# GroupNorm over 128 samples: fifteen small loads added to the SP queue between the last stores

## The chip, the cores and the metric

The kernel runs on one core of one Trainium2 chip. The metric is device time in microseconds (us) of one execution, where lower is better. Besides the timed runs there is one profiled execution of the kernel before; every number read from a view belongs to that execution.

## What is computed

The reference normalises each of 128 samples in 32 groups of 32 channels with 32x16 pixels, and then scales and shifts each channel. Input and output are bfloat16, `x` of 128x1024x32x16, `g` and `b` of 1024.

```python
def reference(x, g, b):
    G = 32
    B, C, H, W = x.shape[0], x.shape[1], x.shape[2], x.shape[3]
    xr = x.reshape(B, G, C // G, H, W)
    mu = xr.mean(axis=(2, 3, 4), keepdims=True)
    var = ((xr - mu) ** 2).mean(axis=(2, 3, 4), keepdims=True)
    xn = (xr - mu) / jnp.sqrt(var + 1e-5)
    xn = xn.reshape(B, C, H, W)
    return xn * g[None, :, None, None] + b[None, :, None, None]
```

## The kernel before

**Tiling.** One tile holds 4 samples times 32 groups, which makes 128 partitions, and each partition holds one whole group: 32 channels of 512 pixels, 16384 bfloat16 values, 32 KB. So there are NT = 32 tiles of 4 MB, and each is loaded once, normalised in place and stored once. Six buffers (`SLOTS` = 6) are used in turn; tile `i` lives in slot `(i + FIRST) % 6` with `FIRST` = 4.

**The compute engines.** For each tile TensorE adds up the 32 blocks of 512 columns by multiplying them with a unit matrix (L209, L193). ScalarE takes a rough mean of the first channel (L217) and sums squared differences from it in four instructions of 4096 columns (L228). VectorE makes mean, variance and the scale and shift of each channel from these (L244 to L284) and rewrites the tile with 32 instructions of 512 columns (L294). The last of the 32 raises the slot's semaphore `done`.

**The DMA program.** Every DMA is issued by SP, in program order, on one queue. SP issues the load of tile 0, two loads that bring `g` and `b` to 128 partitions (L148 and L149; 128 rows of 64 bytes each, one semaphore for both), and the loads of tiles 1 to 5. Then, for each tile `i`, it waits for `done` and issues the store (L141); from tile 1 to tile 26 it also waits until the store of tile `i - 1` has landed and then issues the load of tile `i + 5` into that slot (L136). Stores 27 to 31 have no load between them. Each load and each store has one semaphore per slot that rises by 16 when the DMA has landed. SP waits for nothing else: it is an instruction stream of its own, and what stands behind a waiting instruction on SP is issued later.

**The end.** Behind the last store SP raises `gone` (L156), for which GpSimd waits before it clears the range of the kernel's semaphores (L334), and then SP waits for the landing of the last store of each slot (L158). Behind that come only the few instructions with which the program ends.

The store and load steps in the code:

```python
for i in range(NT):
    store(i)
    if i >= 1 and i + SLOTS - 1 < NT:
        load(i + SLOTS - 1)
sp.sem_inc(s_gone, 1)
```

Of the kernel before, what the change touches and what calls it, by code (L numbers as in the profile page):

```python
# [11 lines left out]
BF16 = mybir.dt.bfloat16  # L12
# [10 lines left out]
def kernel(  # L23
# [20 lines left out]
    NT = B0 // NS  # L44
# [8 lines left out]
    x_v = x.rearrange("(t n) (q k) h w -> t (n q) (k h w)", n=NS, q=G)  # L53
# [8 lines left out]
    def sb(name, shape, dtype):  # L62
        return ctx.enter_context(nc.sbuf_tensor(name, shape, dtype))
# [3 lines left out]
    def sem(name):  # L67
        all_sems.append(nc.alloc_semaphore(name))
        return all_sems[-1]
# [16 lines left out]
    ja = sb("ja", [P, HW], BF16)  # L86
    js = sb("js", [P, SQ], BF16)
    jd = sb("jd", [P, MM_FREE], BF16)
    jv = sb("jv", [P, SQ_PARTS], F32)

    def small(name, n=1):
# [13 lines left out]
    def sems(name):  # L105
        return [sem(f"{name}{j}") for j in range(SLOTS)]
# [11 lines left out]
    s_scl = sems("scl")  # L118
    s_bia = sems("bia")
    s_done = sems("done")  # L120
    s_gb = sem("gb")
    s_gbf = sem("gbf")
    s_eps = sem("eps")
# [6 lines left out]
    sp, pe, act, dve, pool = nc.sync, nc.tensor, nc.scalar, nc.vector, nc.gpsimd  # L130

    def load(i):
        j, n = (i + FIRST) % SLOTS, i // SLOTS
        if n > 0:
            sp.wait_ge(s_store[j], 16 * n)
        sp.dma_start(out=xs[j][:], in_=x_v[i]).then_inc(s_load[j], 16)  # L136

    def store(i):
        j, n = (i + FIRST) % SLOTS, i // SLOTS
        sp.wait_ge(s_done[j], n + 1)  # L140
        sp.dma_start(out=o_v[i], in_=xs[j][:]).then_inc(s_store[j], 16)  # L141
# [10 lines left out]
    for i in range(NT):  # L152
        store(i)
        if i >= 1 and i + SLOTS - 1 < NT:
            load(i + SLOTS - 1)
    sp.sem_inc(s_gone, 1)  # L156
    for j in range(SLOTS):
        sp.wait_ge(s_store[j], 16 * len(range((j - FIRST) % SLOTS, NT, SLOTS)))  # L158
# [6 lines left out]
        out=half[:],  # L165
        in_=ones[:],
# [8 lines left out]
        out=eye[:],  # L175
        in_=half[:],
# [188 lines left out]
```

## Time and profile before

| | |
|---|---|
| three timed runs | 632.34, 633.8 and 633.92 us; median 633.8 us |
| the profiled execution, its own time | 633.28 us |
| its span, first to last instruction | 631.6 us |
| outside the span | 1.68 us |
| queue of the SP DMAs: share of the 16 DMA engines' span | 98.9% |
| bytes read and written | 134.23 MB and 134.22 MB, 425 GB/s over the span |
| ScalarE / VectorE / TensorE busy | 519.4 / 394.9 / 287.4 us |

How to read it: a busy share is an average over the span, and an engine that is 82% busy can still have time to spare at the end. The core's DMAs are carried by 16 DMA engines. The trace holds, for each packet that one of these engines moved, its start, its size and its duration, though not which engine moved it; a tile's row is one packet of 32 KB, so each engine carries 8 packets of each tile. It also holds each increment by which a DMA engine reports to the DMA's semaphore that its part has landed: 16 increments for each load and store. In the groups of the page, "SPq" is SP's instruction stream, and an issue's duration is the time in which SP handled that one instruction; the transfer itself comes later.

### The profile page before, as it was taken

To read this page: it belongs to the slowest core of one execution; us is meant where nothing else is said; L and a number is where in the kernel's file an instruction comes from. 1 tells how busy PE (TensorE), PEld (TensorE's weight loads), DVE (VectorE), ACT (ScalarE), POOL (GpSimd) and SP (SyncE) were. 2 spreads that over 40 slices of the span, in tenths; PEclk is the share of its full clock that TensorE was granted. 3 is DMA by queue.
4 is the path that set the end of the run, shared out by engine and by line. 5 is a ranking of instruction groups with operands and counts; after the bars stand their busy time and mean duration, and the time that the engine had idled before them with its cause. 6 is when DMAs were issued, how large, how long until landed. Compare 5 with 4: busy or idle time off the path is not lost.

```text
span 631.6 us, 2995 instructions
## 1 busy us (share of the span) xinstructions
PE 287.4 (46%) x1024; PEld 3.3 (1%) x32; DVE 394.9 (63%) x1316; ACT 519.4 (82%) x354; POOL 0.8 (0%) x6
## 2 busy tenths in 40 slices
PE   1967605553255532455324654346553455533400
PEld 0000000000000000000000000000000000000000
DVE  0177777666666677777555775556765557755560
ACT  2999999999999999997879887889887898888800
POOL 0000000000000000000000000000000000000000
PEclk9999758756787667876678776777766787667755
DMA  8999999999999999999999999999999999999995
GB/s 363 432 430 417 436 436 432 430 430 434 428 432 432 432 432 432 430 432 430 430 434 434 436 432 432 438 434 436 430 431 434 434 432 432 434 432 432 432 432 235
DMA packets 9484, 268.50 MB, mean 425 GB/s; under 512 B 1288, under 2 KB 1288, under 8 KB 1288
## 3 DMA queue, kind: packets, MB, share of 16 engines
q1 hardware_dynamic: 9480, 268.46, 98.9%
q14 instruction: 3, 0.02, 0.0%
q8 instruction: 1, 0.02, 0.0%
HBM read 134.23 MB, written 134.22 MB: 425 GB/s over the span
## 4 chain that ended last, share of the span: by engine, by line
DMA 73%; ACT 18%; DVE 4%; issue 1%; SPq 1%; DVEq 0%; ACTq 0%
DMA out_dram<-x 67%; ACT js L228 17%; DMA x<-in_x_dram 7%; DVE x L294 3%; ACT ja L217 1%; SPq L136 1%; ACT std L237 0%; DVE jv L268 0%; DVE nd L259 0%; DVE d L255 0%; DVE bia L284 0%; DVE scl L280 0%; DVEq L58 0%; DVE rstd L278 0%; DVEq L254 0%
## 5 line engine op out<-in xcount | busy, mean ns | idle before, releaser
L228 ACT ACTIVATE js<-x,nshift 128x4096 bf16<-128x4096 bf16 x128 | 474.7, 3708 | 4.1
L294 DVE TENSOR_SCALAR x<-x,scl,bia 128x512 bf16<-128x512 bf16 x1024 | 333.7, 406 | 1.2
L193 PE MATMUL ps<-x,eye 128*128 128x512 bf16 x992 | 275.3, 447 | 0.0
L209 PE MATMUL ps<-x,eye 128*128 128x512 bf16 x32 | 18.6, 581 | 303.8 <-DMA x<-in_x_dram 303.8
L255 DVE TENSOR_TENSOR d<-negmean,nshift 128x1 f32<-128x1 f32 x32 | 5.1, 159 | 167.7 <-ACT js L228 167.7
L217 ACT ACTIVATE ja<-x 128x512 bf16<-128x512 bf16 x32 | 20.0, 624 | 48.7 <-DMA x<-in_x_dram 48.0
L244 DVE TENSOR_SCALAR_CACHE_REDUCE jd<-ps 128x512 bf16<-128x512 f32 x32 | 22.0, 686 | 16.4 <-PE ps L193 16.3
L237 ACT ACTIVATE std<-var,eps_t 128x1 f32<-128x1 f32 x32 | 9.4, 295 | 25.8 <-DVE jv L268 25.8
L228 ACT ACTIVATION_READ_ACCUMULATOR js<-x,nshift 128x1 f32 x128 | 23.9, 186 | 0.0
L278 DVE RECIPROCAL rstd<-std 128x1 f32<-128x1 f32 x32 | 5.2, 164 | 11.6 <-ACT std L237 11.6
L284 DVE SCALAR_TENSOR_TENSOR bia<-scl,negmean,bet 128x32 f32<-128x32 f32 x32 | 8.1, 252 | 1.1
L280 DVE TENSOR_SCALAR scl<-gam,rstd 128x32 f32<-128x32 f32 x32 | 7.7, 241 | 1.1
L186 DVE CAST gam<-gam_b 128x32 f32<-128x32 bf16 x1 | 0.2, 181 | 12.9 <-DMA bet_b<-in_b_dram 12.9
L268 DVE TENSOR_SCALAR_CACHE_REDUCE jv<-sq,nd 128x4 f32<-128x4 f32 x32 | 7.0, 217 | 1.1
L259 DVE TENSOR_SCALAR nd<-d 128x1 f32<-128x1 f32 x32 | 6.8, 214 | 1.1
L209 PEld LDWEIGHTS ps<-x,eye 128*128 128x128 bf16 x32 | 3.3, 103 | 578.7 <-DMA x<-in_x_dram 578.7
L217 ACT ACTIVATION_READ_ACCUMULATOR ja<-x 128x1 f32 x32 | 6.0, 187 | 0.0
L268 DVE DVE_READ_ACCUMULATOR jv<-sq,nd 128x1 f32 x32 | 2.7, 83 | 0.0
L244 DVE DVE_READ_ACCUMULATOR jd<-ps 128x1 f32 x32 | 2.6, 82 | 0.0
L184 ACT ACT_TABLE_LOAD x1 | 1.3, 1283 | 1.0 <-ACTq L58 1.0
L161 DVE MEMSET eps_t<- 128x1 f32 x1 | 0.1, 59 | 1.1 <-ACTq L58 1.1
L164 POOL TENSOR_SCALAR_AFFINE_SELECT half<-ones 128x128 bf16<-128x128 bf16 x1 | 0.3, 292 | 0.9 <-DVE ones L162 0.9
(8 smaller groups left out, 1.2 us busy)
## 6 DMA issues: line engine op xcount, KB each, us to landing
x<-in_x_dram SPq DMA_DIRECT2D x32, 4096.0 KB, 29.2
out_dram<-x SPq DMA_DIRECT2D x32, 4096.0 KB, 38.3
gam_b<-in_g_dram SPq DMA_DIRECT2D x1, 8.0 KB
bet_b<-in_b_dram SPq DMA_DIRECT2D x1, 8.0 KB
```

The source lines that it names most:

```text
L136: sp.dma_start(out=xs[j][:], in_=x_v[i]).then_inc(s_load[j], 16)
L193: return pe.add_instruction(mybir.InstMatmult(name=nc.get_next_instruction_name(), ins=[pe.lower_ap(rhs), first.ins[1]], outs=[first.outs[0]],
L209: m = pe.matmul(out=ps[j][:], lhsT=eye[:], rhs=xs[j][:, 0:MM_FREE], start=True, stop=False)
L217: act.activation(out=ja[:], in_=xs[j][:, 0:HW], func=ACT.Identity, scale=-1.0 / HW, accum_out=nshift[j][:],).then_inc(s_shift[j], 1)
L228: act.activation(out=js[:], in_=xs[j][:, k * SQ : (k + 1) * SQ], func=ACT.Square, bias=nshift[j][:], scale=1.0, accum_out=sq[j][:, k : k + 1],
L237: act.activation(out=std[j][:], in_=var[j][:], func=ACT.Sqrt, bias=eps_t[:], scale=1.0).then_inc(s_std[j], 1)
L244: dve.tensor_scalar(out=jd[:], in0=ps[j][:], scalar1=-inv_n, scalar2=None, op0=ALU.mult, op1=ALU.add, accum_out=negmean[j][:],).then_inc(s ...
L259: dve.tensor_scalar(out=nd2[j][:], in0=d[j][:], scalar1=d[j][:], scalar2=-1.0, op0=ALU.mult, op1=ALU.mult,).then_inc(s_nd2[j], 1)
L268: dve.tensor_scalar(out=jv[:], in0=sq[j][:], scalar1=inv_n, scalar2=nd2[j][:], op0=ALU.mult, op1=ALU.add, accum_out=var[j][:],).then_inc(s ...
L280: dve.tensor_scalar(out=scl[j][:], in0=gam[:], scalar1=rstd[j][:], scalar2=None, op0=ALU.mult).then_inc(s_scl[j], 1)
L284: dve.scalar_tensor_tensor(out=bia[j][:], in0=scl[j][:], scalar=negmean[j][:], in1=bet[:], op0=ALU.mult, op1=ALU.add,).then_inc(s_bia[j], 1)
L294: v = dve.tensor_scalar(out=xs[j][:, k * HW : (k + 1) * HW], in0=xs[j][:, k * HW : (k + 1) * HW], scalar1=scl[j][:, k : k + 1], scalar2=bi ...
```

## The change

Right behind the store of tile 28 (`NT - 4`), which is the fourth store from the end, SP issues fifteen loads. Load number `k` brings the first 32 values (64 bytes) of the first `k` rows of tile 0 into a tensor of its own, `k` partitions by 32 values. Together these are 120 rows of 64 bytes. No instruction reads the fifteen tensors. Each load has a semaphore of its own. SP waits for these fifteen semaphores behind the store of tile 31, ahead of raising `gone`. The semaphores lie in the range that GpSimd clears at the end. Nothing is removed, and the order of all the other instructions on all engines stays as it was.

```diff
@@ -86,6 +86,7 @@
     jd = sb("jd", [P, MM_FREE], BF16)
+    few = [sb(f"few{k}_", [k, 32], BF16) for k in range(1, 16)]
     jv = sb("jv", [P, SQ_PARTS], F32)
@@ -118,6 +119,7 @@
     s_done = sems("done")
+    s_few = [sem(f"few{k}_") for k in range(1, 16)]
     s_gb = sem("gb")
@@ -153,6 +155,11 @@
         store(i)
         if i >= 1 and i + SLOTS - 1 < NT:
             load(i + SLOTS - 1)
+        if i == NT - 4:
+            for k in range(1, 16):
+                sp.dma_start(out=few[k - 1][:], in_=x_v[0][0:k, 0:32]).then_inc(s_few[k - 1], 16)
+    for v in s_few:
+        sp.wait_ge(v, 16)
     sp.sem_inc(s_gone, 1)
```

## The prediction

> **What bounds the kernel now.** I read the page's 40 slices first, then the chain that ended last, then SP's waits and issues from 540 us on, and last the DMA packets of two short stretches. A change of 0.3% (1.9 us) either way is about what a measurement of this kernel can tell from none.
>
> ```profile
> DMA  8999999999999999999999999999999999999995
> ...
> DMA packets 9484, 268.50 MB, mean 425 GB/s; under 512 B 1288, under 2 KB 1288, under 8 KB 1288
> ...
> DMA 73%; ACT 18%; DVE 4%; issue 1%; SPq 1%; DVEq 0%; ACTq 0%
> ```
>
> The DMA engines are over 90% busy in every slice but the first and the last, and DMA makes up 73% of the chain. The queue never runs dry: the bytes set the pace. SP is not what is late, as its own waits from 540 us on show (line, waited for: us, times, longest):
>
> ```profile
> SPq L141 <- DVE x L294: 55.3, 3, 19.0
> SPq L158 <- DMA out_dram<-x: 19.5, 3, 9.6
> ```
>
> SP waits three times for a tile from VectorE (stores 29, 30, 31), up to 19.0 us each, and at the end 19.5 us for stores to land. Yet these late issues cost nothing: store 31 is issued at 610.27 us, and the increments of store 30 still land from 613.85 to 620.57 us. Everything issued from 553 us on stands behind some four tiles of transfers, of about 9.7 us each.
>
> The end has a shape of its own. This is the DMA view of the last 10 us (each column 0.25 us):
>
> ```profile
> DMA  9966033360309003090003600030000000000000
> GB/s 524 786 262 262 0 131 131 131 262 0 131 0 393 0 0 131 0 393 0 0 0 131 262 0 0 0 131 0 0 0 0 0 0 0 0 0 0 0 0 33
> DMA packets 48, 1.02 MB, mean 102 GB/s; under 512 B 16, under 2 KB 16, under 8 KB 16
> ```
>
> The full rate ends near 623 us, and then single packets trickle on. The trace's increments say the same: of store 31's sixteen, eleven land between 623.52 and 624.09 us, and the other five at 625.10, 627.40, 629.17, 629.32 and 630.24. **The end is set by one DMA engine that is 6.7 us behind the first**; SP's last wait ends at its 630.24. Its lag can be followed back through all 64 tile transfers, since it is always at least 0.7 us more than the second slowest's from the second on (2.2 us at load 1, 3.6 at 72 us, 6.5 at 333 us). So work added to that engine's share moves the end by its whole length, and work of up to 0.9 us on any other engine moves nothing.
>
> **The change part by part.** It removes nothing. It adds fifteen issues on SP, 120 rows of 64 bytes with their increments in the queue, fifteen waits on SP, and fifteen semaphores to clear.
>
> *Issues on SP.* The rows nearest to them are SP's first DMAs (start, duration) and store 28 with the store behind it:
>
> ```profile
> 0.98 0.39 SPq L136 DMA_DIRECT2D x<-in_x_dram  x1
> 1.43 0.72 SPq L148 DMA_DIRECT2D gam_b<-in_g_dram  x1
> 2.20 0.56 SPq L149 DMA_DIRECT2D bet_b<-in_b_dram  x1
> 2.81 9.10 SPq L136 DMA_DIRECT2D x<-in_x_dram  x5
> ...
> 553.74 18.14 SPq L141 DMA_DIRECT2D out_dram<-x  x2
> ...
> 571.54 0.33 SPq L141 DMA_DIRECT2D out_dram<-x  x1
> ```
>
> Store 28 is issued at 553.74 us (0.50 us), and store 29 waits for VectorE until 571.54: 17.3 us in which SP does nothing. Fifteen issues cost between 15 x 0.33 = 5.0 us (the shortest store) and 15 x 0.72 = 10.8 us (the `g` load). I take 0.56, the later of the two 64-byte-row loads: 8.4 us. They end at 562.6 us and are hidden under VectorE's work on tile 29. One issue went otherwise: the first of the five loads at 2.81 took 6.34 us, right behind 256 rows of 64 bytes. By rows, 120/256 of that is 3.0 us, and 8.4 + 3.0 = 11.4 us still fits. If every small load were held for 6.34 us, SP would come to store 29 only at 554.2 + 95.1 = 649 us, and the end would be near 680: that is the far bound. I set it aside since the loads issued right behind the 6.34 took 1.21, 0.44, 0.44 and 0.49 us, with more in flight each time.
>
> With that cover gone there is a second one. Behind store 28 the queue holds work until its own landing (594.49 us for the first engine, 601.20 for the slowest), so store 29 may be issued as late as some 594 us, 22 us after its place now, before any engine runs dry.
>
> *Packets.* The fifteen loads stand behind store 28 and ahead of store 29 in the queue, and a load of `k` rows needs `k` packets of 64 bytes and some increments. The stretch where one DMA engine begins to move the rows of `g`, 12.43 to 12.50 us, in columns of 1.75 ns:
>
> ```profile
> DMA  0030003000300030003000700930003000300070
> ...
> DMA packets 13, 0.03 MB, mean 477 GB/s; under 512 B 12, under 2 KB 12, under 8 KB 12
> ```
>
> A small packet starts every fourth column, so every 7 ns, with no gap for a read or a write to come back. The whole of `g` and `b`, 256 rows and 8 increments, is through between 12.43 and 13.44 us. The record has ten increments for the two loads: two at 2.53 and 3.18 us, right behind their issue, and eight with the data, four for each load. So four DMA engines carried them, 66 packets each. If one engine gets a row of every one of the fifteen loads, it gets 15 rows and 15 increments: 30 x 7 = 210 ns. Does the slowest engine get them? At load 1, right behind `g` and `b`, the four that are latest (0.61, 0.70, 1.38 and 2.19 us) stand apart from the rest (up to 0.41), as four that had 66 small packets, 0.47 us, more would. So the slowest is likely one of the four that `g` and `b` used. If the small loads begin with the same ones, it gets 12 to 15 of the fifteen: 0.17 to 0.21 us, **0.2 us**. If it is none of them, the cost is 0.
>
> *What the 7 ns may hide.* In `g` one increment followed 32 rows; now one follows each row on the busiest engine. Upper bound: two engines of the four report `g` at 13.10 and 13.21 us, and `b`, 33 packets later, at 13.34 and 13.45, each 0.24 us on. So one increment can't hold up what is behind it for more than 0.24 us, and fifteen not more than 3.6 us. The lower bound is 0. I take the 7 ns, for a second row speaks for it: the slowest engine's increments for stores 30 and 31 are 9.67 us apart, with 8 packets of median 1.213 us between them (9.70 us), so an increment among large packets leaves no gap at all.
>
> A rule that speaks against this: the Trainium skill, "DMA: Bandwidth & Descriptors", section "Anatomy of one DMA", puts a fixed cost of about 2.0 us on each DMA. Taken as a price of the queue it would make 15 x 2.0 = 30 us, an end near 664 us. The same section says that most of it is the delay until the completion is reported, and the row of `g` and `b` agrees: two whole DMAs passed one engine in 0.47 us.
>
> Which engine gets how much is told by the same page, section "Why a DMA increments its semaphore by 16 and not by 1": a load of `k` rows goes to the lowest-numbered `k` engines. No view of this trace numbers the engines; by the rule the first one would have 15 rows.
>
> *Waits and clearing.* SP's fifteen waits stand behind store 31's issue (610.27 + 0.33 us). By then the small loads have landed (about 601.4 us). Semaphore instructions of L158 take 17 to 28 ns: 15 x 0.028 = 0.42 us, up to 1.1 us with the 0.07 us between neighbours at the end. This lies beside store 30's landing, for which SP now waits until 620.59 us. `gone` comes 0.4 to 1.1 us later, and with it the range clear, 0.59 us at 610.7, some 18 us before the end. Cost 0; without that cover 1.1 us.
>
> **Sum.** 633.28 (span 631.6 plus 1.68 around it) + 0.2 = 633.5 us for this execution. The median of the three runs is 633.8, which is 0.5 above the execution, and the changed kernel is timed in such runs: 633.8 + 0.2 = **634.0 us**.
>
> **Rivals.**
>
> *A small load holds its engine (slower).* If an increment right behind a 64-byte row has to wait for that row to land, and the next row waits for it, the place is the slowest engine's queue between stores 28 and 29. At the bound of 0.24 us a pair, 15 pairs make 3.6 us: 637.4. At the full delay from the last increment's packet (629.90) to its landing (630.24), 0.34 us, it is 5.1 us: 638.9. It decides from 1.9 / 15 = 0.13 us a pair. For it: this pattern is not in the trace. Against it: the 7 ns, and the missing gap.
>
> *SP is held until the queue is dry.* If the fifteen loads fill something that holds SP past 601.2 us, the slowest engine idles. Starting again costs 1.0 us from issue (0.98) to the first packet (2.01 us) and about 0.6 us for the longer first packet (1.79 against 1.21): some 635.6 us, and more the longer SP is held. For it: the 6.34 us issue. Against it: SP had eight DMAs in flight then and went on, and the hold would have to last 47 us.
>
> *Faster.* The lag of 6.7 us grew by chance-like steps; if another execution has 2 us less, the time falls below 632. The runs (632.34 to 633.92) show no such fall, and nothing in the change makes one.
>
> *The change does nothing at all*, because the slowest engine gets no small rows: 633.8 us, inside the forecast.
>
> **How the numbers follow.** Forecast, with the loads that do nothing: 0.74, 632.3 to 635.5. Held engine: 0.15. SP held: 0.06. Faster by over 0.3%: 0.05. So faster 0.05, same 0.74, slower 0.15 + 0.06 = 0.21. The range goes from 632.3, the lowest run, to 637.4, the bound of 0.24 us a pair; left out are the dearer part of the held engine, the longer holds of SP and the faster case, under 0.2 together.
>
> **What would show it.** Right: fifteen small issues of 0.3 to 0.7 us between 554.2 and 566 us on SP; store 29 still issued right behind VectorE's last instruction on its tile; small packets between store 28's and store 29's on each engine at some 7 ns; the lag of the last engine up by 0.2 us at most between these two stores; no wait worth naming for the small loads. Wrong: the last engine's lag jumping by microseconds there, or store 29 issued after 590 us, or other engines joining the late five.

## The result and the profile after

The changed kernel takes 633.91 us (median of 20 runs, 633.34 to 637.66) against 632.32 us of the kernel before in the same measurement (20 runs, 631.55 to 634.04). The ratio is 1.0026, with a 95% interval of 1.0018 to 1.0034, so the change costs 1.6 us (1.1 to 2.1). That is within 0.3%, as forecast, but it is clear of zero, and the working had 0.2 us. That the forecast's 634.0 us was met so closely is luck: the cost was 1.4 us higher than worked out, and the kernel before now came out 1.5 us lower than the 633.8 that the prediction started from. With either error alone it would have been about 1.5 us off.

The profiled execution of the changed kernel took 634.31 us with a span of 632.6 us, 1.0 us longer than before. Its DMA totals, from the page:

```profile
DMA packets 9725, 268.51 MB, mean 424 GB/s; under 512 B 1528, under 2 KB 1528, under 8 KB 1528
```

240 small packets are new, 120 rows and 120 increments. SP's issues and waits around them (start, duration; then who waited for whom, in total, times, longest):

```profile
552.60 0.96 SPq L143 DMA_DIRECT2D out_dram<-x  x2
553.60 9.31 SPq L160 DMA_DIRECT2D few_<-in_x_dram  x15
570.93 0.37 SPq L143 DMA_DIRECT2D out_dram<-x  x1
```

```profile
SPq L143 <- DVE x L301: 46.2, 3, 19.2
SPq L165 <- DMA out_dram<-x: 20.5, 3, 9.6
```

The fifteen issues fill 9.3 us of a stretch in which SP waited for VectorE anyway; store 29 is still issued when VectorE is done. SP's wait for VectorE shrinks from 55.3 to 46.2 us, by just these 9 us, and its wait for the last stores grows from 19.5 to 20.5: the microsecond sits in the DMA engines. The DMA view of the last 10 us shows it:

```profile
DMA  9999096060630306303063033330033300000000
GB/s 524 786 393 393 0 524 262 0 262 0 262 131 0 131 0 262 131 0 131 0 262 131 0 131 131 131 131 0 0 131 131 131 0 0 0 0 0 0 0 0
```

Before, the last packets were thinly spread and the last one started at 628.5 us; now several engines are late together, with packets up to about 630 us. Where it happened is told by the trace's increments (first, and last, of the sixteen of each store, us):

```
             before             after
store 28     594.49 .. 601.20   594.42 .. 600.90
store 29     604.18 .. 610.89   604.39 .. 612.05
store 31     623.52 .. 630.24   623.75 .. 631.37
```

In the kernel before the last engine needs 9.69 us from store 28 to store 29. Now it needs 11.16, and after that the old 9.7 again: 1.47 us are lost once, where the small loads stand. The last engine was 0.3 us earlier at store 28 in this execution, so the end moves by 1.13 us from 630.24.

The small packets themselves run as forecast. A stretch in which one engine moves its rows, 600.55 to 600.72 us, in columns of 4.25 ns:

```profile
DMA  1911011011011010110110110110119190110190
...
DMA packets 31, 0.20 MB, mean 1161 GB/s; under 512 B 25, under 2 KB 25, under 8 KB 25
```

A row and an increment follow every three columns, so a pair takes 13 ns, and 12 pairs are through by 600.71 us. But their increments land far more slowly. Of this engine's twelve loads (those of 4 to 15 rows) they land at

```
601.08 601.27 601.45 601.63 601.83 602.02 602.21 602.40 602.59 602.77 602.95 603.13
```

that is every 0.186 us, fourteen times the pitch of the packets. This is the row that the trace of before did not have.

The large packets behind the small ones say the same. A packet of 32 KB lasts 1.21 us, and in the kernel before none that starts between 594 and 606 us lasts more than 1.25. In the changed kernel six that start between 599 and 606 us do (start, duration, us):

```
600.11 1.96    602.06 1.81
600.24 2.17    602.41 1.70
600.72 1.90    602.61 1.76
```

In each line the second packet starts where the first ends, so each line is one engine. The last line starts right behind the twelve pairs that were through by 600.71 us: this engine takes up the next tile while its small loads are still being reported (until 603.13), and its two packets last 1.2 us longer than two ordinary ones. With the 0.16 us of the small packets that is 1.4 of the 1.47 us lost.

### The profile page after: what moved, and what is told of

Same layout as the page of the kernel before. It is cut to its first block, busy times and chain, and to the rows that moved or that the text cites. A ratio compares the mean times of both kernels' runs of the same rounds, so it can differ in the third digit from the quotient of the medians.

```text
span 632.6 us, 3001 instructions
## 1 busy us (share of the span) xinstructions
PE 288.0 (46%) x1008; PEld 3.3 (1%) x32; DVE 394.9 (62%) x1316; ACT 519.3 (82%) x354; POOL 0.8 (0%) x6
## 4 chain that ended last, share of the span: by engine, by line
DMA 73%; ACT 18%; DVE 4%; issue 1%; SPq 1%; DVEq 0%; ACTq 0%
DMA out_dram<-x 66%; ACT js L235 17%; DMA x<-in_x_dram 7%; DVE x L301 3%; ACT ja L224 1%; SPq L138 1%; ACT std L244 0%; DVE jv L275 0%; DVE nd L266 0%; DVE d L262 0%; DVE bia L291 0%; DVE scl L287 0%; DVEq L58 0%; DVE rstd L285 0%; DVEq L261 0%
## 5 line engine op out<-in xcount | busy, mean ns | idle before, releaser
L251 DVE TENSOR_SCALAR_CACHE_REDUCE jd<-ps 128x512 bf16<-128x512 f32 x32 | 21.9, 685 | 15.6 <-PE ps L200 15.5
```

What stands on the lines that cost most here:

```text
L251: dve.tensor_scalar(out=jd[:], in0=ps[j][:], scalar1=-inv_n, scalar2=None, op0=ALU.mult, op1=ALU.add, accum_out=negmean[j][:],).then_inc(s ...
```

## The experiments

The theories, with the numbers that the profile after suggested:

- **A**: on one DMA engine, increments of successive small loads are held about 0.18 us apart. The engine goes on with the packets behind them meanwhile, which hides the first 0.8 us or so; only the rest is lost. An engine with n pairs loses n x 0.18 - 0.8 us.
- **B**: each small row has a price of about 0.12 us, whatever stands behind it.
- **C**: the cost is in SP's fifteen issues, semaphores and waits, not in the DMA engines.
- **D** (formed after the first four runs): a fixed price of 0.13 us for each pair, with nothing hidden.

All variants change only the number, the shape or the place of the loads (the runs with thirty and with eight loads also let two unused outputs share their space, to make room). Shown of the code are the lines that matter, against the kernel before. Where a loss is named "between stores 28 and 29", it is the mean, over the sixteen increments in order, of the time from store 28 to store 29 less the 9.68 us of the kernel before.

**Two loads of 128 rows.**

```diff
+    rows = [128] * 2
+    few = [sb(f"few{k}_", [n, 32], BF16) for k, n in enumerate(rows)]
...
+        if i == NT - 4:
+            for k, n in enumerate(rows):
+                sp.dma_start(out=few[k][:], in_=x_v[0][0:n, 0:32]).then_inc(s_few[k], 16)
```

> Two loads of 128 rows of 64 bytes instead of the fifteen, at the same place: every DMA engine gets 16 rows but only 2 increments. Theory A (each increment behind small rows holds the writing side of its engine for about 0.18 us until the rows have landed, of which the first 0.8 us in a row are hidden): 2 x 0.18 is below 0.8, so only the packets themselves, 18 x 7 ns = 0.1 us; 0.0 to 0.3 us over the kernel before. Theory B (each small row costs its engine some 0.12 us, whatever stands behind it): 16 x 0.12 = 1.9 us over the kernel before.

Ratio 1.0006 (0.9997 to 1.0015): +0.4 us, -0.2 to 0.9. The loss between stores 28 and 29 is 0.13 us. Sixteen rows on every engine cost next to nothing when only two increments stand behind them: B falls.

**Fifteen loads of 16 rows.** As above, with `rows = [16] * 15`.

> Fifteen loads of 16 rows each: every DMA engine gets 15 rows and 15 increments. Theory A: 15 x 0.18 - 0.8 = 1.9 us over the kernel before, on the late engines and on the others alike; their first landings of store 29 move by as much as the last. Theory B: 15 x 0.12 = 1.8 us. Theory C (the cost is in the fifteen issues, semaphores and waits of SP, not in the engines): as the changed kernel, 1.6 us, and no shift of the landings between stores 28 and 29.

Ratio 1.0037 (1.0025 to 1.0050): +2.3 us, 1.6 to 3.2. The loss is 1.98 us, the first increment moves by 1.95 and the last by 2.00: every engine loses the same. As many rows on each engine as in the run before, less one, but fifteen increments instead of two.

**Five loads of 16 rows.** `rows = [16] * 5`.

> Five loads of 16 rows each: every DMA engine gets 5 rows and 5 increments. Theory A: 5 x 0.18 = 0.9 us on the writing side, nearly all of it hidden: 0.1 to 0.2 us over the kernel before. Theory B (a price for each row, nothing hidden): 5 x 0.12 = 0.6 us. Theory C: a third of 1.6, 0.5 us.

Ratio 1.0004 (0.9995 to 1.0012): +0.25 us, -0.3 to 0.8. By itself that excludes neither 0.1 nor 0.5 us; the trace's loss of 0.16 us does tell, and is A's.

**Fifteen loads of one row.** `rows = [1] * 15`.

> Fifteen loads of one row each: if a load of k rows uses the first k engines, always the same first one, a single engine gets 15 rows and 15 increments, and SP issues, waits and clears exactly as in the changed kernel. Theories A and B: that engine loses 1.9 us; in the changed kernel's profile the engine with all fifteen pairs landed among the first ones, with 5 to 6 us to spare, so the end does not move: 0.0 us (up to 1.9 us in an execution in which that engine happens to be the last). Theory C (issues, semaphores, waits): 1.6 us, as the changed kernel.

Ratio 1.0001 (0.9992 to 1.0010): +0.1 us, -0.5 to 0.6. SP issues, waits and clears as often as in the changed kernel, and nothing is lost: C falls. One engine alone reports the fifteen loads. In this execution it was not among the first, as I had thought from the changed kernel's profile, but 3.7 us behind them; its increments land from 598.50 to 601.05, 0.182 us apart, and from store 28 (598.32) to store 29 (609.95) it loses 1.95 us. It had 2.8 us to spare, and the end does not move. This one engine gives the numbers of A more sharply: 15 x 0.182 = 2.73 us of holds, 1.95 of them lost, so **0.78 us hidden**. Its next large packet starts at 598.18 us, when none of the fifteen has been reported, and lasts 2.36 us, the one behind it 1.74, and then they last 1.21 again. So the engine does go on meanwhile; that this is what hides the 0.78 us fits, but no run tests it by itself.

**Thirty loads of 16 rows.** `rows = [16] * 30`.

> Thirty loads of 16 rows each, so 30 rows and 30 increments on every DMA engine; to make room, the unused output of the rough mean shares the space of the unused output of the squares. Theory A (0.182 us for each pair on the writing side, the first 0.78 us hidden): 30 x 0.182 - 0.78 = 4.7 us later between stores 28 and 29 on every engine, and as much over the kernel before. Theory D (a fixed price of 1.95 / 15 = 0.13 us for each pair, nothing hidden): 3.9 us.

Ratio 1.0094 (1.0079 to 1.0110): +5.9 us, 5.0 to 7.0. The loss is 4.71 us against A's 4.7 and D's 3.9. The timed runs show more than that. In the profile the last engine lost 5.18 us, and its increments were 0.19 us apart, which makes 30 x 0.19 - 0.78 = 4.9; the remainder of about a microsecond (0.1 to 2.1) is open. SP was not the reason in this profile, although its issues grew long:

```profile
L161 SPq DMA_DIRECT2D few_<-in_x_dram x30: 422/926/2949, 552.6 to 586.6; - x30
```

The columns are the shortest, median and longest issue in ns. From the 22nd on they take 1.5 to 2.9 us, and stores 29 and 30 are issued at 589.1 and 591.1 us, 18 us late for store 29, yet before any engine has run dry.

**One load of 16 rows behind each of fifteen stores.**

```diff
         store(i)
+        if 12 <= i < 27:
+            k = i - 12
+            sp.dma_start(out=few[k][:], in_=x_v[0][0:16, 0:32]).then_inc(s_few[k], 16)
         if i >= 1 and i + SLOTS - 1 < NT:
```

> Fifteen loads of 16 rows, as in the run that cost 2.3 us, but one behind each of the stores 12 to 26 instead of all behind store 28. Theory A: a single hold of 0.18 us is below the 0.78 us that are hidden, and the 9.7 us until the next one let the writing side catch up: only the packets, 15 x 0.013 = 0.2 us over the kernel before. Theory D (a fixed price for each pair, wherever it stands): 1.95 to 2.3 us.

Ratio 1.0010 (1.0001 to 1.0019): +0.6 us, 0.1 to 1.2. The same fifteen loads that cost 2.3 us in a row cost 0.6 when they are spread, one every 19.4 us; the interval takes in A's 0.2 and excludes D's 1.95. The trace agrees: from store 11 to store 28 the increments take 319.85 us on the mean, against 319.80 in the kernel before (319.67 to 319.96 in the runs that change nothing in this stretch). So the hidden part is there for each hold anew when they stand apart.

**Fifteen loads of 128 rows.** `rows = [128] * 15`.

> Fifteen loads of 128 rows of 64 bytes: 15 increments on every DMA engine as with 16 rows, but 120 rows. Theory A (the increments are held): successive increments 0.21 us apart, as in the run with two loads of 128 rows, so 15 x 0.21 - 0.78 = 2.4 us over the kernel before. Theory B (each row has its price): 120 x 0.13 = 15.6 us. If SP is held by so many rows, its issues take longer than 0.6 us each, but have 40 us before an engine runs dry.

Ratio 1.0043 (1.0029 to 1.0057): +2.7 us, 1.8 to 3.6. Eight times the rows of the run with 16, and nowhere near B's 15.6 us. It is not a clean test of A, though. The 0.21 us that the expectation took from the run with two loads is not what the last engine showed there, which was 0.19. Here the last engine's increments are 0.18 to 0.20 us apart but for two gaps of 0.43 and 0.37 us, whose reason is open; it loses 2.84 us instead of 2.4. And the first increment of store 29 comes 6.4 us late for another reason: SP is held.

```profile
L161 SPq DMA_DIRECT2D few_<-in_x_dram x15: 328/434/10706, 551.8 to 599.0; - x15
```

The fifth load takes 10.7 us to issue, the next three 8.5 each and the ninth 6.1, so store 29 is issued only at 599.4 us, when the early engines have nothing left but a few small loads. These engines had slack, and the end does not show it.

**Fifteen loads of 16 rows behind the last store.** `if i == NT - 1`.

> The fifteen loads of 16 rows behind the last store instead of the fourth from the end, where nothing comes behind them that could be read ahead. Theory A: nothing is hidden, and the last engine's fifteenth increment lands 15 x 0.182 = 2.7 us after its increment of store 31; then the raising of gone and the range clear of 0.6 to 0.7 us come behind it, which were beside the stores before: 3.4 to 4.0 us over the kernel before. Theory D: 15 x 0.13 = 1.95 us to the fifteenth increment, 2.6 to 3.2 us over the kernel before.

Ratio 1.0064 (1.0050 to 1.0078): +4.0 us, 3.2 to 4.9. The last engine reports store 31 at 629.37 us and its fifteen small loads from 629.55 to 632.18, 2.81 us: nothing is hidden behind the last store. In SP's waits of this kernel the small loads now stand at the end:

```profile
SPq L163 <- DMA few_<-in_x_dram: 9.3, 2, 9.1
```

The range clear (0.68 us) comes behind them, at 632.3 us. Both parts are as A had them; D had 1.95 us for the fifteen increments, and 2.6 to 3.2 us in all.

**Rows of 2 KB and of 64 bytes.** The runs so far don't say what an increment is held for: the landing of the row before it (A1), or merely a distance from the increment before (A2).

```diff
+    few = sb("few_", [P, 1024], BF16)
...
+        if i == NT - 4:
+            for k in range(8):
+                r = slice(16 * k, 16 * k + 16)
+                sp.dma_start(out=few[r, :], in_=x_v[0][r, 0:1024]).then_inc(s_few[k], 16)
```

> Eight loads of 16 rows of 2 KB, each into 16 partitions of one shared tensor: 8 rows of 0.076 us (1.213 us / 16) and 8 increments on every DMA engine; the unused output of the rough mean shares the space of the unused output of the squares. Theory A1 (an increment waits until the row in front of it has landed, and the next row waits for it): the row's transfer comes on top, so increments land 0.076 + 0.18 = 0.26 us apart, and the engines lose 8 x 0.26 - 0.78 = 1.3 us between stores 28 and 29. Theory A2 (two increments of one engine can't be closer than 0.18 us, whatever is between them): 0.18 us apart, and 8 x 0.18 - 0.78 = 0.7 us, hardly more than the 0.61 us that the bytes take.

The second kernel of the pair has `[P, 32]` and `0:32` instead.

> The same eight loads with rows of 64 bytes, for comparison. Theories A1 and A2: increments 0.18 us apart, and 8 x 0.18 - 0.78 = 0.7 us lost between stores 28 and 29, 0.7 us over the kernel before. Theory D (0.13 us a pair, nothing hidden): 1.0 us.

Rows of 2 KB: ratio 1.0010 (1.0001 to 1.0019), +0.6 us, 0.1 to 1.2; loss 0.78 us. Rows of 64 bytes: 1.0018 (1.0009 to 1.0028), +1.1 us, 0.6 to 1.8; loss 0.72 us (the timed runs allow D's 1.0 as well, the loss does not). The last engine's increments, from the trace:

```
rows of 2 KB:      600.68 600.87 601.05 601.23 601.42 601.60 601.79 601.99
rows of 64 bytes:  601.78 601.98 602.16 602.34 602.53 602.71 602.90 603.08
```

Both are 0.186 us apart, although a packet of 2 KB lasts 0.084 us and one of 64 bytes 0.011. The row's transfer does not come on top: A1 falls as it was stated, and A2's distance holds for rows up to 2 KB. Why two increments of one engine keep this distance stays open. So does whether the price belongs to the increment or to something else that comes once for each DMA on an engine, for in all these runs each small DMA gave an engine one increment and no more.

Put together (loss between stores 28 and 29 in the trace, against n x 0.182 - 0.78):

```
increments in a row on each engine     5      8      15     30
loss in the trace, us                  0.16   0.72   1.98   4.71
n x 0.182 - 0.78, us                   0.13   0.68   1.95   4.68
```

The two constants come from the single engine of the run with one-row loads; the other numbers of the table are not fitted. The changed kernel, whose sixteen engines have 15, 14, ... 1 and 0 pairs, is one more test: the formula, with nothing lost up to four pairs, gives a mean loss of 0.72 us, D gives 120 x 0.13 / 16 = 0.98, and the trace has 0.80. Single engines scatter: one with 11 pairs lost 1.58 us there instead of 1.22.

## Why the prediction was right, and which term was mis-sized

**The bound.** Right: the DMA queue sets the pace, and the end is set by the one DMA engine that is furthest behind. Work on its share moved the end; fifteen pairs on another engine moved nothing (one-row loads).

**Issues on SP.** Right: 9.3 us of issues instead of 8.4, inside the 17 us that SP waited. The second cover held as well: in the run with thirty loads store 29 went out 18 us late and no engine ran dry. The rival "SP is held until the queue is dry" is real in kind: fifteen loads of 128 rows do hold SP, for 6 to 11 us in five of the issues. The changed kernel's 120 rows do not.

**Packets.** The 7 ns was right as the pitch at which packets start (13 ns for a pair), and wrong as the price. **The step that failed is "What the 7 ns may hide"**: I took 7 ns for an increment that the runs show at 0.182 us. The upper bound of 0.24 us, from `g` and `b`, held, and the true distance lies close to it. For that choice I named two rows, and neither can carry it. Packet starts tell when an engine takes a packet up, increments when it reports it as landed, and here twelve pairs were taken up within 0.16 us and reported within 2.2 us. The 0.47 us in which two whole DMAs "passed one engine" is counted from starts as well. And the missing gap between stores 30 and 31 shows only that a single hold each 9.7 us costs nothing, which is what the run with spread loads confirms. Fifteen in a row are another matter: the first 0.78 us are covered, the rest is not.

The Trainium skill, "DMA: Bandwidth & Descriptors", section "Anatomy of one DMA", has two figures on either side of this: about 2.0 us of fixed cost for a DMA, and a bubble of about one cycle for the semaphore write. The section describes DMAs that GpSimd issues, which the prediction did not say; those of this kernel are issued by SP. As prices in this queue neither agrees with the runs, where the increments of small DMAs in a row came 0.182 us apart.

**Which engine.** The slowest engine was said to be one of the four that `g` and `b` use, and to get 12 to 15 pairs. The increments of the changed kernel's four late engines tell how many pairs each had: 14, 11, 12 and 5. By the Trainium skill, "DMA: Bandwidth & Descriptors", section "Why a DMA increments its semaphore by 16 and not by 1", a load of `k` rows uses the lowest-numbered `k` engines; counting so, these four are numbers 1, 4, 3 and 10 from 0, and the counts fit (a load of `k` rows is reported by `k` engines each time). So two of the late ones are not among the first four, and the engine with all fifteen was not late. The last one had 12 pairs, at the low end of my 12 to 15: 12 x 0.182 - 0.78 = 1.40 us, where 1.47 was lost. That it had so many is partly luck, for which engines are late is not the same in each execution: the one that gets all fifteen was among the first in the changed kernel's profile and 3.7 us behind them in that of the one-row loads.

**Waits and clearing.** Right: SP's waits for the small loads run from 610.32 to 610.75 us, and the range clear takes 0.68 us at 610.8, all beside the last stores. Behind the last store, where that cover is gone, both stand on the path.

**The rivals.** The slower one, "a small load holds its engine", is what happened, at a lower price: the hold is 0.18 us, between its 0.13 and its 0.34, but 0.78 us of it are hidden, which leaves 0.12 us a pair on the last engine. That is just under the 0.13 from which it would have decided, and so the time stayed within 0.3%. Its mechanism is not shown: the row's transfer does not come on top of the hold, and what the increment waits for stays open.

**The sum.** 0.2 us in the prediction; 1.5 us between stores 28 and 29 in the profile, 1.6 us (1.1 to 2.1) in the timed runs. The prediction's own signs say so too: the lag between these stores grew by 1.47 us and not by 0.2 at most, and other engines joined the late five (eight land store 31 after 624.5 us, where five did), which it had named as a sign of being wrong. And twenty runs of each kernel tell 0.5 us, where it had counted on 1.9.

## What to carry to other kernels

On this busy queue small DMAs were priced by how many of their completions fell on one DMA engine in a row, not by their bytes (rows of 64 bytes and of 2 KB) or rows (one or eight on an engine): among transfers of 4 MB the first four or so were free, and each further one cost 0.18 us. Spread them between large transfers, or join them into few DMAs, and keep them away from the end, where nothing hides them. And when a trace shows packets without gaps, look at when their increments land, and at how long the next large packet lasts, before calling them cheap: starts show only when an engine takes them up.

## What was not expected of the hardware

- Increments that one DMA engine reports for successive small DMAs land 0.18 to 0.19 us apart on a late engine, with one row of 64 bytes or of 2 KB between them; with 8 rows of 64 bytes between them (two loads of 128 rows) it is 0.18 to 0.19 us as well.
- After such a group among 4 MB transfers the engines have lost, on the mean, about 0.75 us less than distances of 0.182 us add up to, in groups of 5, 8, 15 and 30. The packet of 32 KB behind the group lasts longer for it: 2.36 us instead of 1.21 behind fifteen small loads on one engine.
- SP's issue of a small load took 0.25 us (median) with one row and, with 16 rows, 0.44 in five loads and 0.56 in fifteen; late in a longer group SP was held for 1.5 to 2.9 us an issue (thirty loads of 16 rows) and 6 to 11 us (fifteen of 128).
